# Two phase sums moved between the sixth and the seventh product, and a flag read ahead of the last work, in a gated linear attention with a cosine-gated layer

## The chip, the core and the metric

The kernel runs on one NeuronCore of a Trainium2 chip. The metric is the device time of one execution in microseconds (us), as a median over runs. All times below are in us unless marked ns. The engines are named as the profile names them: PE is TensorE's matmul and PEld its weight load, DVE is VectorE, ACT is ScalarE, POOL is GpSimd and SP is SyncE; a "q" behind the name marks the engine's sequencer or, for a DMA, the queue that issues it.

## The reference

Two blocks are computed one after the other. The first is a recurrence over 768 steps with a complex decay for each of 4 batches and 8 heads; the head size is 48:

```python
mag = np.sqrt(a_re * a_re + a_im * a_im)
scale = np.minimum(mag, 0.999) / (mag + 1e-06)
a_re_n, a_im_n = (a_re * scale, a_im * scale)
for t in range(S):
    ar, ai = (a_re_n[:, :, t, :, None], a_im_n[:, :, t, :, None])
    new_re = ar * S_re - ai * S_im
    new_im = ar * S_im + ai * S_re
    kv = np.einsum('bhd,bhe->bhde', k[:, :, t], v[:, :, t])
    S_re, S_im = (new_re + kv, new_im)
    y[:, :, t] = np.einsum('bhd,bhde->bhe', q[:, :, t], S_re)
```

Its result, as 3072 rows of 384 columns, goes through a layer with weights of 384 x 2048 and 2048 x 384:

```python
h = x @ w_in
g = h * np.cos(h)
return g @ w_out
```

## The kernel before

**Tiles and groups.** The steps are cut into chunks of 128 and two chunks make a group, so there are 12 groups (NG). One iteration n of the main loop in `fast_path` (from L1542 on) weaves three groups together: the scores, states and outputs of group n, the second matrix product of group n-1, and the decays, angles and keys of group n+1. The iteration ends with the first matrix product of group n (its "gate sums", named hp in the profile) and its gates.

**The angles of a group (n+1).** `log_steps` makes the logarithm and the angle of each decay on ScalarE and VectorE. `p_powers` and `g_phase` then sum them over the steps with matmuls by triangular matrices. `g_phase` (phs in the profile) does six matmuls for the two chunks of a group, then a cast on ScalarE and a subtraction on VectorE (both write tan). `keys` follows: `g_trig` (sine and cosine on ScalarE), `g_stack` (four products on VectorE: ks and qs), and `f_transpose` for the keys and then for the queries. Each `f_transpose` is one transpose on VectorE (tr), one copy to DRAM on SyncE's queue (moved) and the loads back: four for the keys (kT), one for the queries (qT). The transpose of the queries is put behind the first gate product of the previous group (`behind(turn, X[g - 1]["gated"])`). The next group's scores (sc) read kT and qT.

**The second product in seven.** From group 2 on (PLAIN) a group's second product is made as seven half-size products (`seventh`, p = 0 to 6, each in two parts of four j) after a Strassen-like scheme; `mixes` makes the mixed operands on VectorE. Products p = 0, 3, 5, 6 add into one PSUM tile (sum), the others use another (op). After each product ScalarE or VectorE adds it into the output tile ot. The product p = 6, the seventh, adds into sum, so it must wait until ScalarE has read out the state after p = 5, the sixth. In the last group p = 6 has a tile of its own (`alone`).

**What sets the order.** TensorE's matmuls are chained in the order in which the code calls them (`matmul` with `chain`). `weave` sorts the calls of an iteration by a number: each part spreads its items evenly over a span, as in

```python
(products(n - 1, 3, 7), 0.4, 0.56), (phases(n + 1), 0.472, 0.476),
(keys(n + 1), 0.5, 0.62), (quarters() if n == PLAIN else [], 0.4, 0.9),
```

so that both phases stand between the fifth product (its second part is at 0.47) and the sixth (at 0.49). In this stage VectorE's, ScalarE's and SyncE's instructions are ordered by a planner, which works with its own costs and takes what is ready, with the order of the code as priority; `behind` adds an edge that keeps one instruction after another on its engine. Each engine then runs its queue in order.

**The end.** `least`, `odd` and `wide` gather checks of the inputs' range. At the end of `tile_gateloop__then__act_gcu_kernel` (L1553 on) VectorE reduces them to one number for each partition, two DMAs write them into a line in DRAM, one reads the line back into one partition, VectorE reduces it to a flag, and every engine reads the flag (L1592) and branches on it (L1594). With the flag set the slow `general_path` would be run after all; with these inputs it is jumped over. All stores of the output are on SyncE's queue, so that SyncE reads the flag after the last store.

Of the kernel before, what the change touches and what calls it, by code (L numbers as in the profile page):

```python
# [11 lines left out]
F32 = mybir.dt.float32  # L12
U8 = mybir.dt.uint8
U32 = mybir.dt.uint32
I32 = mybir.dt.int32
# [4 lines left out]
ALU = mybir.AluOpType  # L20
AX = mybir.AxisListType
# [463 lines left out]


@with_exitstack
def fast_path(ctx, tc, q, k, v, a_re, a_im, moe_w_in, moe_w_out, out, least, odd, wide):

# [3 lines left out]
    nc = tc.nc  # L495
    B, H, S, D = q.shape
    DM, DF = moe_w_in.shape
    C = 128
# [3 lines left out]
    NG = N // G  # L502
    D2 = 2 * D
# [147 lines left out]
    late = {}  # L651
    tail = {}
# [33 lines left out]
    vector, scalar = Ordered(nc.vector, "vector"), Ordered(nc.scalar, "scalar")  # L686
# [424 lines left out]
    def quarters():  # L1111

        for name in "s1", "s2", "a22":
            right[name] = stage["pool"].tile([C, HJ, E2], F32, name="t_" + name)
        t1, t2, t4 = (right[name] for name in ("s1", "s2", "a22"))
        for j in range(0, HJ, 2):
            for t, a, b in (t1, b12, b11), (t2, b22, t1), (t4, b21, t2):
                yield lambda t=t, a=a, b=b, j=j: behind(vector.tensor_tensor(
                    out=t[:, ds(j, 2)], in0=a[:, ds(j, 2)], in1=b[:, ds(j, 2)],
                    op=ALU.subtract), Y[PLAIN * G]["masked"])  # L1120
# [28 lines left out]
    def seventh(g, p, part):  # L1149


        x, name = X[g], SEVEN[p]
        if p == 0 and part == 0:
            x["sum"] = pm.tile([C, E2], F32, tag="acc", name="sum", bufs=1)
            x["ot"] = [msb.tile([C, DM], F32, tag="ot", name="ot") for _ in range(G)]

        alone = g == NG - 1 and p == 6
        summed = p in (0, 3, 5, 6) and not alone
        if not summed and part == 0:
            x["op"] = pm.tile([C, E2], F32, tag="m", name="op", bufs=2)  # L1160
        ps = x["sum"] if summed else x["op"]
        for j in range(part * HJ // 2, (part + 1) * HJ // 2):
            matmul(ps, lhsT=left(g, name, j), rhs=right[name][:, j],
                   start=(j == 0 and (p == 0 or not summed)),
                   stop=(j == HJ - 1), skip_group_check=summed)
        if part == 0:
            return
        c11, c12, c21, c22 = (x["ot"][i][:, ts(half, E2)] for i in range(2) for half in range(2))
        if p in (0, 2, 5) or p == 6 and not alone:
            scalar.mul(out={0: c11, 2: c21, 5: c22, 6: c12}[p], in_=ps, mul=scale)  # L1170
        if g == NG - 1 and p == 5:
            scalar.mul(out=c12, in_=ps, mul=scale)
        if p in (1, 3, 4, 5) or alone:
            part_ = {1: c11, 3: c21, 4: c21, 5: c22, 6: c12}[p]
            added = vector.scalar_tensor_tensor(out=part_, in0=x["op"] if p == 5 else ps, scalar=scale,
                                                in1=part_, op0=ALU.mult, op1=ALU.add)
        row = g * G * C
        if g == NG - 1 and p == 1:
            nc.sync.dma_start(out=out[ds(row, C), 0:E2], in_=c11)
        elif p == 5:  # L1180
            late["out"] = added
            nc.sync.dma_start(out=out[ds(row + C, C), :], in_=x["ot"][1])
        elif p == 6:
            nc.sync.dma_start(out=out[ds(row, C), ds(alone * E2, DM - alone * E2)],
                              in_=c12 if alone else x["ot"][0])

    def products(g, lo, hi):
        if g < PLAIN:
            return []
        return [lambda p=p, part=part: seventh(g, p, part)  # L1190
                for p in range(lo, hi) for part in range(2)]

    def mixes(g, lo, hi):
        return [lambda p=p: mixed(g, p) for p in range(lo, hi)] if g >= PLAIN else []

    def weave(*parts):

        items = []
        for p, (part, lo, hi) in enumerate(parts):
            part = list(part)  # L1200
            items += [(lo + (hi - lo) * (i + 0.5) / len(part), p, t)
                      for i, t in enumerate(part)]
        for _, _, t in sorted(items, key=lambda x: x[:2]):
            t()
# [4 lines left out]
    def keys(g):  # L1209

        if not 0 <= g < NG:
            return
        for i, n in spans(g):
            yield lambda i=i, n=n: g_trig(g, i, n)
            yield lambda i=i, n=n: (g_stack(g, i, n), p_end(g, i, n))
            for name in "kT", "qT":
                if g >= PEG:
                    yield lambda i=i, n=n, name=name: f_transpose(g, i, n, name)
# [21 lines left out]
    def phases(g):  # L1240
        return [lambda i=i: g_phase(g, i) for i in range(G)] if 0 <= g < NG else []
# [299 lines left out]
    for n in range(2, NG):  # L1541
        weave((mixes(n - 1, 2, 4), 0.0, 0.12), (logs(n + 1), 0.0, 0.02), (chunks(n), 0.0, 0.36),  # L1542
              (upper[2:] if n == 2 else [], 0.0, 0.2), (products(n - 1, 0, 3), 0.0, 0.36),
              (prods(n + 1), 0.25, 0.27), (second(n - 1, 1), 0.36, 0.5),
              (products(n - 1, 3, 7), 0.4, 0.56), (phases(n + 1), 0.472, 0.476),
              (keys(n + 1), 0.5, 0.62), (quarters() if n == PLAIN else [], 0.4, 0.9),
              (last_quarter() if n == PLAIN else [], 0.9, 1.0), (first(n), 0.56, 1.0),
              (mixes(n, 0, 2), 0.9, 1.0), (guarded(n - 1, per) if n > 3 else [], 0.1, 0.9))
    weave((mixes(NG - 1, 2, 4), 0.0, 0.1), (products(NG - 1, 0, 7), 0.0, 1.0))
    assert not guards  # L1550
    return late
@with_exitstack
def kernel(ctx, tc, q, k, v, a_re, a_im, moe_w_in, moe_w_out, out):  # L1553

    nc = tc.nc
    D2, H = 2 * q.shape[3], q.shape[1]
    keep = ctx.enter_context(tc.tile_pool(name="keep", bufs=1))
    least = keep.tile([D2, 2 * H], F32, name="least")  # L1560
    C = 128
    NG, NJ = q.shape[0] * q.shape[2] // C // 2, moe_w_out.shape[0] // C
    odd = keep.tile([C, moe_w_in.shape[0] // C * 4 + NJ + NG + 1], F32, name="odd")
    wide = keep.tile([C, NG * NJ // 2], F32, name="wide")
    late = fast_path(tc, q, k, v, a_re, a_im, moe_w_in, moe_w_out, out, least, odd, wide)
    low = keep.tile([D2, 1], F32, name="low")
    nc.vector.tensor_reduce(out=low, in_=least, axis=AX.X, op=ALU.min)
    even = keep.tile([C, 1], F32, name="even")
    nc.vector.tensor_reduce(out=even, in_=odd, axis=AX.X, op=ALU.max)
    most = keep.tile([C, 1], F32, name="most")  # L1570
    nc.vector.tensor_reduce(out=most, in_=wide, axis=AX.X, op=ALU.max)
    nc.vector.tensor_scalar(out=even, in0=even, scalar1=0.0, scalar2=None, op0=ALU.is_le)
    nc.vector.tensor_scalar(out=most, in0=most, scalar1=2.4, scalar2=None, op0=ALU.is_le)
    nc.vector.tensor_tensor(out=even, in0=even, in1=most, op=ALU.mult)
    scratch = ctx.enter_context(tc.tile_pool(name="scratch", bufs=1,
                                             space=bass.MemoryType.DRAM))
    line_d = scratch.tile([D2 + C], F32, name="line_d")

    def behind(ins, other):
        tc.add_manual_dep(ins.ins, other.ins.name, mybir.DependencyInfo(  # L1580
            mybir.DependencyClass.NoSync, mybir.DependencyReason.DATA))

    behind(nc.sync.dma_start(out=line_d[0:D2], in_=low.rearrange("p o -> (p o)")),
           late["x"])
    nc.sync.dma_start(out=line_d[D2:D2 + C], in_=even.rearrange("p o -> (p o)"))
    line = keep.tile([1, D2 + C], F32, name="line")
    nc.sync.dma_start(out=line, in_=line_d.unsqueeze(0))
    bad = keep.tile([1, 2], F32, name="bad")
    behind(nc.vector.tensor_reduce(out=bad[:, 0:1], in_=line, axis=AX.X, op=ALU.min), late["out"])
    flag = keep.tile([1, 1], I32, name="flag")  # L1590
    nc.vector.tensor_scalar(out=flag, in0=bad[:, 0:1], scalar1=0.5, scalar2=None, op0=ALU.is_lt)
    taken = nc.values_load(flag[0:1, 0:1], min_val=0, max_val=1,  # L1592
                           skip_runtime_bounds_check_because="a comparison gives 0 or 1")
    with tc.If(taken > 0):  # L1594
        general_path(tc, q, k, v, a_re, a_im, moe_w_in, moe_w_out, out)


# [28 lines left out]
```

## Time and profile before

| | |
|---|---|
| median of 3 runs | 666.53 (664.78 to 667.04) |
| the profiled execution | 666.49 |
| its span, from the first to the last instruction | 664.7 |
| granted TensorE clock, mean | 0.996 |
| gate sums of one group (hp, 96 matmuls) | 20.7 |
| one of the seven products (16 matmuls) | 2.6 from start to start |
| both phase sums of a group (6 matmuls) | 1.05 |
| last matmul's end to the span's end | 6.8 |

The profile is one execution. Matmuls are pipelined and their ends are modelled, so the distance from the start of one product to the start of the next is the better measure of a product. A group of instructions is told as `line engine operation out<-in`, with the tiles by the program's names; as every matmul is issued in one helper, all stand on L689. A wait is put down to the instruction that released it. Reading the flag and branching are work of an engine's sequencer and are not counted as busy.

### The profile page before, as it was taken

Reading aid. Unit: us, or ns where it says so; the run is one execution under the profiler, and the core shown is the slowest. Engines: PE = TensorE matmul, PEld = TensorE weight load, DVE = VectorE, ACT = ScalarE, POOL = GpSimd, SP = SyncE. Lnnn points to the kernel's source line nnn. Section 1 sums busy time; section 2 is a strip of 40 time slices with the busy share of each in tenths; the row PEclk is TensorE's granted clock in tenths of the full one; section 3 lists DMA queues with packets and bytes.
Section 4 is the critical chain, followed back from the end, with each engine's and each line's share of the span. In section 5 each row is a group of like instructions: output and inputs, shape, how many; then the busy total and the mean of one; then the engine's idle time right before and its main releaser. Section 6 shows DMA issues by size and latency. Waiting matters only on the chain.

```text
span 664.7 us, 10764 instructions
## 1 busy us (share of the span) xinstructions
PE 644.0 (97%) x4077; PEld 575.7 (87%) x4077; DVE 491.7 (74%) x797; ACT 393.3 (59%) x728; POOL 28.0 (4%) x47
## 2 busy tenths in 40 slices
PE   7899999999999999999999999999999999999995
PEld 5788867767998999899899899898899899899895
DVE  4999989499788688688688688687688778762241
ACT  7888687284673593593594494495486486332330
POOL 2010200000000000010010010000000000000000
PEclk9999999999999999999999999999999999999998
DMA  9968755637628557657648637826927833533000
GB/s 245 207 190 215 211 170 120 166 64 186 132 48 209 124 145 190 143 139 170 166 126 188 164 100 163 214 72 146 240 80 164 206 94 96 164 98 96 25 6 25
DMA packets 233626, 94.90 MB, mean 143 GB/s; under 512 B 208846, under 2 KB 222033, under 8 KB 233564
## 3 DMA queue, kind: packets, MB, share of 16 engines
q1 hardware_dynamic: 227068, 68.62, 45.2%
q0 software_dynamic: 5632, 25.17, 11.4%
q8 instruction: 34, 0.56, 0.4%
q10 hardware_dynamic: 864, 0.33, 0.2%
q14 instruction: 28, 0.23, 0.1%
HBM read 69.28 MB, written 24.81 MB: 142 GB/s over the span
## 4 chain that ended last, share of the span: by engine, by line
PE 83%; DMA 5%; ACT 5%; DVE 5%; issue 1%; POOL 0%; DVEq 0%; SPq 0%; POOLq 0%
PE hp L689 37%; PE op L689 17%; PE sum L689 11%; PE sc L689 5%; PE yp L689 5%; PE sp L689 4%; DMA xT<-x 2%; PE phs L689 2%; DMA raw<-in_moe_w_out_dram 1%; ACT rs L709 1%; DVE tan L678 1%; PE lgs L689 1%; DVE mag L678 1%; ACT lo L709 1%; DMA x<-yT 1%
## 5 line engine op out<-in xcount | busy, mean ns | idle before, releaser
L689 PE MATMUL hp<-xT,w_in 128*128 128x256 f32 (+1 forms) x1176 | 252.7, 375 | 1.4 <-DMA xT<-x 1.4
L689 PEld LDWEIGHTS hp<-xT,w_in 128*128 128x128 f32 x1176 | 219.5, 190 | 32.2 <-DMA xT<-x 2.0
L709 ACT ACTIVATE gate<-hp,half_pi_b 128x512 f32<-128x512 f32 x96 | 66.0, 687 | 120.5 <-PE hp L689 120.5
L678 DVE TENSOR_TENSOR gate<-hp,gate 128x512 f32<-128x512 f32 x96 | 65.8, 685 | 70.3 <-ACT junk L678 69.8
L689 PE MATMUL op<-w_out,gate 128*128 128x192 f32 (+1 forms) x448 | 100.7, 374 | 0.0
L689 PEld LDWEIGHTS op<-w_out,gate 128*128 128x128 f32 x448 | 75.9, 190 | 16.9 <-issue 2.0
L678 ACT ACTIVATE junk<-hp 128x512 bf16<-128x512 f32 x96 | 56.6, 590 | 0.0
L689 PE MATMUL sum<-t_s,s 128*128 128x192 f32 x320 | 55.4, 326 | 0.2 <-DVE ot L678 0.2
L678 DVE TENSOR_TENSOR atm<-sc,causal 128x512 f32<-128x512 f32 x48 | 32.8, 687 | 30.0 <-PE sc L689 30.0
L689 PEld LDWEIGHTS sum<-t_s,s 128*128 128x128 f32 x320 | 52.6, 190 | 0.5 <-DVE ot L678 0.5
L689 PEld LDWEIGHTS sc<-qT,kT 96*128 96x128 f32 x384 | 47.7, 192 | 1.9 <-ACT qT L678 0.5
L689 PE MATMUL sc<-qT,kT 96*128 96x128 f32 x384 | 49.0, 275 | 0.2 <-ACT qT L678 0.2
L678 ACT ACTIVATE ot<-sum 128x192 f32<-128x192 f32 x30 | 9.5, 319 | 45.8 <-PE sum L689 45.8
L689 PE MATMUL yp<-atm,v 128*48 128x128 f32 x352 | 33.6, 277 | 1.1 <-DVE atm L678 1.1
L705 ACT ACT_TABLE_LOAD x24 | 30.8, 1283 | 4.0 <-DMA ident<-ident_const 3.6
L678 ACT CAST tan<-phs 128x384 int32<-128x384 f32 x24 | 11.4, 480 | 36.5 <-PE phs L689 36.5
L689 PE MATMUL sum<-w_out,s 128*128 128x192 f32 x144 | 25.8, 332 | 4.2 <-ACT ot L678 4.2
L689 PEld LDWEIGHTS sp<-v,ks 128*96 128x96 f32 x320 | 29.7, 165 | 0.0
L689 PE MATMUL yp<-qT,state 96*48 96x128 f32 x304 | 29.7, 272 | 0.0
L689 PE MATMUL sp<-v,ks 128*96 128x48 f32 x320 | 29.7, 245 | 0.0
L689 PE MATMUL sum<-w_out,gate 128*128 128x192 f32 x160 | 29.6, 329 | 0.0
L689 PEld LDWEIGHTS sum<-w_out,s 128*128 128x128 f32 x144 | 23.1, 190 | 6.9 <-ACT ot L678 6.9
(138 smaller groups left out, 976.2 us busy)
## 6 DMA issues: line engine op xcount, KB each, us to landing
moved<-tr SPq DMA_DIRECT2D x20, 768.0 KB
raw<-in_moe_w_in_dram POOLq DMA_DIRECT2D x16, 768.0 KB, 5.3
raw<-in_moe_w_out_dram POOLq DMA_DIRECT2D x16, 768.0 KB, 4.9
kT<-moved SPq DMA_DIRECT2D x40, 192.0 KB
qT<-moved SPq DMA_DIRECT2D x10, 768.0 KB
k<-in_k_dram SPq DMA_DIRECT2D x24, 192.0 KB
q<-in_q_dram SPq DMA_DIRECT2D x24, 192.0 KB
v<-in_v_dram SPq DMA_DIRECT2D x24, 192.0 KB
```

The costliest lines, as they stand in the source:

```text
L678: ins = getattr(self.engine, op)(**kw)
L689: chain(nc.tensor.matmul(out, **kw), "tensor")
L705: chain(nc.scalar.preload_act_table_set(table))
L709: chain(nc.scalar.activation(func=func, **kw))
```

## The change

It has two parts. In the main loop, for n = 3 to 10, the two phase sums are called between the sixth and the seventh product, and the keys' steps are called a little later; for n = 2 (PLAIN), where there are no seven products, all stays.

```diff
-              (products(n - 1, 3, 7), 0.4, 0.56), (phases(n + 1), 0.472, 0.476),
-              (keys(n + 1), 0.5, 0.62), (quarters() if n == PLAIN else [], 0.4, 0.9),
+              (products(n - 1, 3, 7), 0.4, 0.56),
+              (phases(n + 1), *((0.472, 0.476) if n == PLAIN else (0.516, 0.524))),
+              (keys(n + 1), *((0.5, 0.62) if n == PLAIN else (0.53, 0.64))),
+              (quarters() if n == PLAIN else [], 0.4, 0.9),
```

The second part is the end. The instructions that make the flag become a generator, `verdict`, which the last weave steps through: the line is made during the first product of the last group, the flag is made and read by all engines after the fourth, and TensorE's read is put behind the first half of the sixth. ScalarE's read is put behind its read-out of an earlier product, VectorE's last addition behind VectorE's read, SyncE's second-last store behind SyncE's read. The store of the first output quarter is put behind the line's read. The last store goes to ScalarE's queue, behind ScalarE's read. The branch itself stays where it was, after each engine's last instruction.

```diff
-    weave((mixes(NG - 1, 2, 4), 0.0, 0.1), (products(NG - 1, 0, 7), 0.0, 1.0))
+    checked = verdict(late)
+
+    def judged():
+        late["tensor"] = tail["tensor"]
+        next(checked, None)
+
+    weave((mixes(NG - 1, 2, 4), 0.0, 0.1), ([judged], 0.05, 0.15),
+          (products(NG - 1, 0, 7), 0.0, 1.0), ([judged], 0.58, 0.6), ([judged], 0.76, 0.8))
...
+            if alone:
+                behind(added, late["read DVE"])
+            late["vector"] = added
         row = g * G * C
         if g == NG - 1 and p == 1:
-            nc.sync.dma_start(out=out[ds(row, C), 0:E2], in_=c11)
+            behind(nc.sync.dma_start(out=out[ds(row, C), 0:E2], in_=c11), late["line"])
         elif p == 5:
-            late["out"] = added
-            nc.sync.dma_start(out=out[ds(row + C, C), :], in_=x["ot"][1])
+            put = nc.sync.dma_start(out=out[ds(row + C, C), :], in_=x["ot"][1])
+            if g == NG - 1:
+                behind(put, late["read SP"])
+        elif p == 6 and alone:
+            behind(nc.scalar.dma_start(out=out[ds(row, C), E2:DM], in_=c12),
+                   late["read Activation"])
         elif p == 6:
-            nc.sync.dma_start(out=out[ds(row, C), ds(alone * E2, DM - alone * E2)],
-                              in_=c12 if alone else x["ot"][0])
+            nc.sync.dma_start(out=out[ds(row, C), :], in_=x["ot"][0])
...
+    def verdict(late):
...
+        late["line"] = nc.sync.dma_start(out=line, in_=line_d.unsqueeze(0))
+        yield
+        bad = keep.tile([1, 2], F32, name="bad")
+        behind(nc.vector.tensor_reduce(out=bad[:, 0:1], in_=line, axis=AX.X, op=ALU.min),
+               late["vector"])
+        flag = keep.tile([1, 1], I32, name="flag")
+        nc.vector.tensor_scalar(out=flag, in0=bad[:, 0:1], scalar1=0.5, scalar2=None,
+                                op0=ALU.is_lt)
+        reads, values = nc.values_load_multi_w_load_instructions(
+            flag[0:1, 0:1], min_val=0, max_val=1,
+            skip_runtime_bounds_check_because="a comparison gives 0 or 1")
+        late["taken"] = values[0]
+        for ins in reads:
+            name = str(ins.ins.engine).split(".")[-1]
+            late["read " + name] = ins
+        behind(late["read Activation"], late["scalar"])
+        yield
+        behind(late["read PE"], late["tensor"])
+
+    late = fast_path(tc, q, k, v, a_re, a_im, moe_w_in, moe_w_out, out, least, odd, wide, verdict)
+    with tc.If(late["taken"] > 0):
         general_path(tc, q, k, v, a_re, a_im, moe_w_in, moe_w_out, out)
```

The instructions at the start of `verdict` (left out at its "...") are the same reductions, comparisons and DMAs that stood behind `fast_path` before.

More of the change, by code (lines that the diff above doesn't have):

```diff
@@ L487, in fast_path @@
 @with_exitstack
-def fast_path(ctx, tc, q, k, v, a_re, a_im, moe_w_in, moe_w_out, out, least, odd, wide):
+def fast_path(ctx, tc, q, k, v, a_re, a_im, moe_w_in, moe_w_out, out, least, odd, wide,
+              verdict):
     nc = tc.nc
@@ L1169, in seventh @@
         if p in (0, 2, 5) or p == 6 and not alone:
-            scalar.mul(out={0: c11, 2: c21, 5: c22, 6: c12}[p], in_=ps, mul=scale)
+            late["scalar"] = scalar.mul(out={0: c11, 2: c21, 5: c22, 6: c12}[p], in_=ps, mul=scale)
         if g == NG - 1 and p == 5:
@@ L1564 @@
     wide = keep.tile([C, NG * NJ // 2], F32, name="wide")
[L1565 to L1574, printed above, removed]
     scratch = ctx.enter_context(tc.tile_pool(name="scratch", bufs=1,
                                              space=bass.MemoryType.DRAM))
-    line_d = scratch.tile([D2 + C], F32, name="line_d")
     def behind(ins, other):
@@ L1581, in behind @@
             mybir.DependencyClass.NoSync, mybir.DependencyReason.DATA))
[L1583 to L1594, printed above, removed]
+    def verdict(late):
+        low = keep.tile([D2, 1], F32, name="low")
+        nc.vector.tensor_reduce(out=low, in_=least, axis=AX.X, op=ALU.min)
+        even = keep.tile([C, 1], F32, name="even")
+        nc.vector.tensor_reduce(out=even, in_=odd, axis=AX.X, op=ALU.max)
+        most = keep.tile([C, 1], F32, name="most")
+        nc.vector.tensor_reduce(out=most, in_=wide, axis=AX.X, op=ALU.max)
+        nc.vector.tensor_scalar(out=even, in0=even, scalar1=0.0, scalar2=None, op0=ALU.is_le)
+        nc.vector.tensor_scalar(out=most, in0=most, scalar1=2.4, scalar2=None, op0=ALU.is_le)
+        nc.vector.tensor_tensor(out=even, in0=even, in1=most, op=ALU.mult)
+        line_d = scratch.tile([D2 + C], F32, name="line_d")
+        behind(nc.sync.dma_start(out=line_d[0:D2], in_=low.rearrange("p o -> (p o)")),
+               late["x"])
+        nc.sync.dma_start(out=line_d[D2:D2 + C], in_=even.rearrange("p o -> (p o)"))
+        line = keep.tile([1, D2 + C], F32, name="line")
+        late["line"] = nc.sync.dma_start(out=line, in_=line_d.unsqueeze(0))
[16 more added lines that the diff above has]
+        behind(late["read PE"], late["tensor"])
```

## The prediction

> **What bounds the kernel now.** I read the page first (shares, then the chain that ended last), then the list of waits, then the timeline of one group and of the end.
>
> ```profile
> PE 644.0 (97%) x4077; PEld 575.7 (87%) x4077; DVE 491.7 (74%) x797; ACT 393.3 (59%) x728; POOL 28.0 (4%) x47
> PE 83%; DMA 5%; ACT 5%; DVE 5%; issue 1%; POOL 0%; DVEq 0%; SPq 0%; POOLq 0%
> ```
>
> TensorE is busy in 97% of the span and is 83% of the chain. So time is won only where TensorE stands still, or after its last matmul. The waits list names the stop between the sixth and the seventh product:
>
> ```profile
> PE sum L689 <- ACT ot L678: 4.2, 9, 0.5
> PE hp L689 <- DMA xT<-x: 1.4, 2, 1.2
> ```
>
> The timeline of one group (the iteration n=4) shows what surrounds it. The columns are start, duration, engine, line and operation; the wait stands at the end.
>
> ```profile
> 249.88 2.76 PE L689 MATMUL op<-w_out,gate 128*128 128x192 f32 x16
> 252.34 0.47 PE L689 MATMUL phs<-hi,exact 128*128 128x384 f32 x1
> ...
> 253.52 2.76 PE L689 MATMUL sum<-t_s,s 128*128 128x192 f32 x16
> ...
> 256.40 0.31 ACT L678 ACTIVATE ot<-sum 128x192 f32<-128x192 f32 x1
> ...
> 256.76 2.87 PE L689 MATMUL sum<-w_out,s 128*128 128x192 f32 x16 [0.48 <-ACT ot L678]
> ...
> 259.47 15.70 PE L689 MATMUL hp<-xT,w_in 128*128 128x256 f32 x72
> 259.53 2.25 DVE L678 STREAM_TRANSPOSE tr<-ks 128x1536 f32<-128x1536 f32 x1
> ...
> 264.16 2.24 DVE L678 STREAM_TRANSPOSE tr<-qs 128x1536 f32<-128x1536 f32 x1
> ...
> 271.58 2.66 SPq L926 DMA_DIRECT2D qT<-moved  x1
> ```
>
> The seventh product (256.76) adds into the bank that ScalarE must first read out (256.40). TensorE has nothing between. The two phase sums (six matmuls, 252.34 to 253.5) stand one product earlier. After the phases a long chain follows: angles, sines, stack, two transposes on VectorE, six DMAs on SyncE's queue, of which qT is last; the next group's first scores (280.19 here) need it.
>
> At the end, the view of the flag's load and branch (lines 1592 and 1594) shows durations in ns and start times:
>
> ```profile
> L1592 PEldq TENSOR_LOAD <-flag x1: 739/739/739, 656.6 to 656.6; - x1
> L1592 SPq TENSOR_LOAD <-flag x1: 521/521/521, 658.8 to 658.8; - x1
> L1594 PEldq COMPARE_BRANCH  x1: 3842/3842/3842, 657.4 to 657.4; - x1
> L1594 SPq COMPARE_BRANCH  x1: 45/45/45, 659.4 to 659.4; - x1
> L1594 SPq EVENT_SEMAPHORE  x8: 17/17/17, 662.5 to 663.0; - x8
> ```
>
> SyncE issues the last store at 658.42, reads the flag at 658.8, branches at 659.4, and its next instruction comes at 662.5: 3.0 us of nothing. Then follow 20 semaphore instructions (1.4) and the closing barrier. From the last matmul (657.9) to the span's end (664.7) it is 6.8 us.
>
> **What the Trainium skill says.** "Runtime: NRT & Kernel Launch", section Instruction fetch mechanics: a taken branch to a target outside the window that is held must fetch instructions by DMA first. The trace agrees: after their branches POOL, ACT, DVE and SP stand 2.5, 2.7, 3.1 and 3.0 us, and instruction blocks of 16 KB move meanwhile. "Advanced Engine Details and Errata", section Engine Queue Depths, gives TensorE's queue 64 entries. The trace shows part of it: the flag's load began on PE's sequencer at 656.58, when matmuls to 657.9 (16 instructions or more) were still to run. "PSUM — Partial Sum Buffer", section PSUM bank collisions, wants a semaphore between a reader and a writer of a bank; the 0.48 us above is such a wait.
>
> **The phases, step by step.** A product takes 2.60 us (start to start, 247.28 to 249.88). From 253.52 two products should end at 258.72, but the gate sums begin at 259.47. So the stop costs 0.75 with its restart. The phase sums take 1.05 wherever they stand. Placed in the stop, they give ScalarE 1.05 us for a read that was done 0.6 after the product; ScalarE has little else then, since the casts and sines of the angles now come later. Gain: up to 0.75 in each of eight groups (n=3 to 10; the waits list counts a ninth, n=11, which has no phases), 6.0 in all.
>
> The price is the chain behind the phases, which starts 2.60 later, and its cover is the slack at the next group's scores. From the trace's semaphore records qT lands at 279.38 and the scores begin at 280.19: slack 0.81. For n=3 to 10 it is 1.75, 0.81, 1.35, 1.65, 2.14, 1.49, 0.92, 1.56. As the gain also moves the scores forward by 0.75, a group's net is -0.75 + max(0, D + 0.75 - slack), where D is how much later qT lands.
>
> D is not 2.60, since part of the chain waits anyway. Phases end at 256.29 instead of 253.69. VectorE's first transpose followed 5.84 after them, of which 0.27 was the addition of the sixth product, now done before: it runs 261.86 to 264.1. The first gate product, ready at 263.56 - 0.75 = 262.8, follows to 264.75, and the second transpose, which the code holds behind that gate, runs to 267.0, against 266.4 before. The first transpose's copy lands 3.3 us after its issue (261.80 to 265.06), so at 267.4, and the kT loads start then instead of at 266.85. D = 0.6. VectorE's lateness has cover: the fourth gate sum (266.5) needs the buffer that the first gate product frees (264.75).
>
> Exceptions: at n=8 the gate sums wait for xT (465.20 landed, 465.24 begun), so nothing is gained; at n=5 xT leaves 0.71. At n=10 SyncE has the kT loads ahead of the second copy, and D could be 2.3 (+0.8); put the other way round it gains 0.75: I take 0. With D = 0.6: -0.75, -0.21, -0.71, -0.75, -0.75, 0, -0.32, 0: sum **-3.5**. Bounds: D = 0.35 (the case at n=8, where an earlier DMA held SyncE) gives -4.7, D = 1.3 (VectorE half a microsecond slower) about -0.2.
>
> **The flag and the last store.** The same eight small VectorE instructions and three DMAs (two writes into a line, one read) are moved, none is removed. They ran beside products at 641.7 to 650 already, costing TensorE nothing. The store of the first quarter is now queued behind the line's read on SyncE: 645.40 becomes about 650.2; only the end waits for it, and it lands before the last ones. The line lands at 652.88; its reduction waited until 656.00 for the sixth product's addition, and now runs at about 652.9.
>
> The loads of the flag then start some 0.57 later, at 653.5. ACT (0.66), DVE (0.54), SP (0.52) and POOL (0.72) have nothing queued behind theirs before 655.4: cost nothing. TensorE's load stands between the halves of the sixth product, which starts at 652.56, so its first half ends at 653.86. Behind the load are queued 24 matmuls and their weights. The load ends at 653.5 + 0.74 = 654.2 at a line as late as now: a stop of 0.3 to 0.65. A line earlier by 1 us (no store in its way) means none. I take 0.3.
>
> After the last matmul: the addition ends 0.47 later (658.39). SyncE's work ends at 656.5 with the second-last store, so its fetch is over by 659.5. VectorE branches at 658.1 instead of 658.7, over by 661.2. ScalarE issues the last store at 658.4 (0.44, as its DMAs at the start took), branches at 658.9 and with its 2.74 goes on at 661.6. The store lands by 661.0, as now. ScalarE is last; its own semaphore, SyncE's last ones and the barrier end 1.1 later, at about 662.75 instead of 664.7: -1.95. With TensorE's stop: **-1.65**. Bounds: -2.3 (no stop, a quicker fetch as POOL's 2.5) and -0.6 (stop 0.65 and a fetch of 3.5).
>
> **Sum.** The profiled execution took 666.49, 1.8 around its span of 664.7; the median of the runs is 666.53, the same. 666.49 - 3.5 - 1.65 = **661.4**; the bounds give 659.5 to 665.7 for this case.
>
> **Rivals.** *The transposes come after the gate.* If VectorE's queue has the first gate product ahead of the first transpose, the latter runs 263.4 to 265.7, its copy lands at 269.0, the second ends at 267.9 and kT starts 2.2 to 2.6 later. TensorE then waits for qT in each group. With D = 2.3: +0.55, 1.49, 0.95, 0.65, 0.16, 0.81, 1.38, 0.74, sum +6.7, and with the end's gain +5.0: 671.5. It decides from D of about 1.65 on, where the groups' loss eats the end's gain. For it: the two are only 0.95 apart in readiness, and the order is a planner's. Against: the transpose is ready first, and before it was ahead by 4. *The stop stays.* If ScalarE's queue has a cast of a phase ahead of the read of the sum, the read ends 1.5 after the product, the seventh waits 0.5 beyond the phases, and only the end gains: 664.8. Against: the read is ready first by half a microsecond. *The end gives nothing.* The load starves TensorE by 0.65 and ScalarE's fetch is as slow as TensorE's 3.84: the end keeps about 0.2, total 662.8.
>
> **Chances.** Likeliest 0.62, transposes behind the gate 0.18, the stop stays 0.10, the end gives nothing 0.10. Range 659.0 to 669.5: it holds all but the worse part of the first rival (D above 2.0) and a gain beyond the bounds. Some 0.3% (2 us) is what a measurement of this kernel can tell from no change. Faster than 664.5: 0.57 of the likeliest, 0.03 and 0.08 of the last two, 0.68; slower than 668.5: 0.14 of the first rival; the rest, 0.18, between.
>
> **What would show it.** Right: no wait of sum on ACT's ot but one, phs between the sums, qT's issue some 0.6 later, scores that wait little, a branch on SP near 656.5, an end some 4.9 after the last matmul. Wrong: a new wait of sc on a DMA of 1 us or more in most groups, a PE gap at the load beyond 0.7, or the 0.48 still there.

## The result and the profile after

The changed kernel takes 660.68 us (median of 22 runs, 658.18 to 667.46), the kernel before 665.77 us in 22 runs on the same chip: ratio 0.9921, 95% interval 0.9902 to 0.9941. It is faster by 5.1 us.

The ratios leave out each kernel's slow runs, so they are not just the quotient of the medians, and some executions begin the main loop 5 to 8 us late (the profiled one of the changed kernel, 667.46 us with a span of 665.7, does), so stretches are counted below from the first gate sums of n=2 (164.41 us after, 156.44 before) to the end.

The page after: the shares of the engines, the granted clock in 40 slices (the 6 in the third falls in the late beginning), and the chain that ended last.

```profile
PE 650.7 (98%) x4077; PEld 582.8 (88%) x4077; DVE 490.6 (74%) x797; ACT 393.5 (59%) x728; POOL 27.9 (4%) x47
...
PEclk9969999999999999999999999999999999999999
...
PE 79%; DMA 7%; DVE 6%; ACT 2%; SPq 2%; issue 2%; POOL 0%; DVEq 0%; POOLq 0%
```

TensorE is still the bound. The list of TensorE's waits after (total, times, longest) has changed where the change was made:

```profile
PE hp L690 <- DMA xT<-x: 0.9, 1, 0.9
...
PE sum L690 <- ACT ot L679: 0.4, 1, 0.4
PE sc L690 <- DMA qT<-moved: 0.3, 1, 0.3
```

Of the nine stops of a sum behind ScalarE's read-out, the eight of n=3 to 10 are gone; the one of n=11 is left. The scores wait anew for qT, 0.28 us at 540.28 (and 0.14 at 388.12, which this list leaves out). The timeline of n=4 after shows the new order (start, duration, engine, line, operation, the idle time before in brackets):

```profile
257.38 2.76 PE L690 MATMUL op<-w_out,gate 128*128 128x192 f32 x16
...
259.98 2.76 PE L690 MATMUL sum<-t_s,s 128*128 128x192 f32 x16
...
262.44 0.47 PE L690 MATMUL phs<-hi,exact 128*128 128x384 f32 x1
...
262.78 0.33 ACT L679 ACTIVATE ot<-sum 128x192 f32<-128x192 f32 x1 [5.78 <-PE sum L690]
...
263.62 2.76 PE L690 MATMUL sum<-w_out,s 128*128 128x192 f32 x16
...
266.22 10.09 PE L690 MATMUL hp<-xT,w_in 128*128 128x256 f32 x46
...
269.36 2.25 DVE L679 STREAM_TRANSPOSE tr<-ks 128x1536 f32<-128x1536 f32 x1
...
271.58 0.68 DVE L679 TENSOR_TENSOR gate<-hp,gate 128x512 f32<-128x512 f32 x1
...
272.19 2.23 DVE L679 STREAM_TRANSPOSE tr<-qs 128x1536 f32<-128x1536 f32 x1
```

The phase sums fill 262.44 to 263.6 while ScalarE reads the sum out (262.78 to 263.11), and the seventh product starts with nothing shown ahead of it. From 259.98, two products of 2.60 and the phases' 1.05 should end at 266.23; the gate sums begin at 266.22, so nothing is lost between. The first transpose still goes ahead of the first gate product, the second behind it.

At the end, the flag's loads and branches after, in ns with start times:

```profile
L1612 SPq TENSOR_LOAD <-flag x1: 482/482/482, 656.1 to 656.1; - x1
...
L1612 PEldq TENSOR_LOAD <-flag x1: 492/492/492, 657.3 to 657.3; - x1
L1612 ACTq TENSOR_LOAD <-flag x1: 471/471/471, 657.9 to 657.9; - x1
```

```profile
L1624 SPq EVENT_SEMAPHORE  x8: 17/17/17, 662.1 to 663.1; - x8
...
L1624 SPq COMPARE_BRANCH  x1: 45/45/45, 659.0 to 659.0; - x1
...
L1624 ACTq COMPARE_BRANCH  x1: 54/54/54, 661.3 to 661.3; - x1
...
L1624 ACTq EVENT_SEMAPHORE  x1: 17/17/17, 664.7 to 664.7; - x1
```

SyncE now branches at 659.0, before TensorE's last matmul ends (660.40), and goes on at 662.1. ScalarE issues the last store at 660.90, branches at 661.3 and goes on at 664.7: it is now last.

Where the time went, from each profile. "n=3-10" is from the gate sums of n=2 to those of n=10; "n=11 on" from there to the last matmul's end; the tail is the rest of the span.

| kernel (main loop's beginning) | n=3-10 | n=11 on | tail | sum |
|---|---|---|---|---|
| before (156.44) | 412.26 | 89.23 | 6.79 | 508.27 |
| before, second profile (164.66) | 411.93 | 92.08 | 6.72 | 510.73 |
| after (164.41) | 407.05 | 88.95 | 5.27 | 501.27 |
| after, second profile (162.81) | 407.98 | 88.92 | 5.41 | 502.31 |
| phases alone (156.24) | 409.90 | 92.31 | 6.82 | 509.03 |
| end alone (156.32) | 411.93 | 89.19 | 4.62 | 505.74 |
| own tile, phases as before (163.59) | 406.37 | 90.23 | 4.75 | 501.35 |
| low's write later (156.26) | 408.16 | 87.77 | 5.10 | 501.03 |
| last store on SyncE (156.27) | 407.94 | 90.18 | 6.87 | 504.99 |
| transposes behind the gate (162.70) | 416.53 | 90.78 | 4.74 | 512.05 |
| own tile, low's write later (163.82) | 406.04 | 87.09 | 5.40 | 498.53 |
| no branch (160.96) | 408.20 | 92.28 | 3.10 | 503.58 |

From before to after the eight groups give 5.2 us, n=11 on 0.3, the tail 1.5.

### The profile page after: what moved, and what is told of

The parts are those of the page before. It is cut to its first block, busy times and chain, and to the rows that moved or that the text cites. A ratio compares the mean times of both kernels' runs of the same rounds, so it can differ in the third digit from the quotient of the medians.

```text
span 665.7 us, 10771 instructions
## 1 busy us (share of the span) xinstructions
PE 650.7 (98%) x4077; PEld 582.8 (88%) x4077; DVE 490.6 (74%) x797; ACT 393.5 (59%) x728; POOL 27.9 (4%) x47
## 4 chain that ended last, share of the span: by engine, by line
PE 79%; DMA 7%; DVE 6%; ACT 2%; SPq 2%; issue 2%; POOL 0%; DVEq 0%; POOLq 0%
PE hp L690 31%; PE op L690 17%; PE sum L690 13%; PE sc L690 5%; PE yp L690 5%; PE sp L690 3%; PE phs L690 2%; DMA qT<-moved 2%; SPq L925 2%; PE lgs L690 1%; DMA raw<-in_moe_w_out_dram 1%; DMA xT<-x 1%; DVE mag L679 1%; PE yr L690 1%; DVE qs L679 1%
## 5 line engine op out<-in xcount | busy, mean ns | idle before, releaser
L690 PE MATMUL hp<-xT,w_in 128*128 128x256 f32 (+1 forms) x1176 | 255.3, 378 | 0.9 <-DMA xT<-x 0.9
L690 PEld LDWEIGHTS hp<-xT,w_in 128*128 128x128 f32 x1176 | 222.2, 193 | 31.9 <-DMA xT<-x 1.4
L679 DVE SCALAR_TENSOR_TENSOR ot<-op,ot 128x192 f32<-128x192 f32 x31 | 11.0, 355 | 33.8 <-ACT ot L679 24.8
L690 PE MATMUL op<-t_a,gate 128*128 128x192 f32 x160 | 29.0, 332 | 0.0
L679 ACT COPY yT<-yp 48x512 f32<-48x512 f32 x44 | 25.3, 574 | 4.7 <-PE yp L690 4.3
```

The costliest lines, as they stand in the source:

```text
L679: ins = getattr(self.engine, op)(**kw)
L690: chain(nc.tensor.matmul(out, **kw), "tensor")
```

## The experiments

The theory: filling the stop in eight groups gives some 3.5 us, less than the stop cost because qT's lateness gives part back; the early flag and ScalarE's queue give about 1.65. The rivals: one part does it all, the order of the transposes decides, or the stop could have been removed for more without moving the phases.

The experiments ran on several chips, so each is to be read by its ratio to the kernel before on its own chip. There the kernel before takes 671.34 us beside the phases alone, the end alone, the own tile and low's later write, and 669.48 beside the other four.

### Each part alone

The phases alone: the kernel before with the first hunk of the diff.

```diff
-              (products(n - 1, 3, 7), 0.4, 0.56), (phases(n + 1), 0.472, 0.476),
-              (keys(n + 1), 0.5, 0.62), (quarters() if n == PLAIN else [], 0.4, 0.9),
+              (products(n - 1, 3, 7), 0.4, 0.56),
+              (phases(n + 1), *((0.472, 0.476) if n == PLAIN else (0.516, 0.524))),
+              (keys(n + 1), *((0.5, 0.62) if n == PLAIN else (0.53, 0.64))),
+              (quarters() if n == PLAIN else [], 0.4, 0.9),
```

> The kernel before with the phases and keys moved, the end as before. Theory (each stop of 0.75 us before the seventh product is filled, the chain behind the phases is covered by the slack at the next scores): 3.5 to 5.5 us less than before, ratio 0.992 to 0.995; the wait of sum on ACT's ot falls from 9 to 1; the end stays at 6.8 us after the last matmul. Rival (the gain of the change is mostly the end): less than 2 us, ratio above 0.997.

Measured 666.73 us, ratio 0.9937 (0.9905 to 0.9969). In its profile n=3-10 takes 409.90, 2.4 us less than before; n=11 on takes 3.1 us more than before: 1.6 of that is a longer wait for xT (2.8 us against 1.2), and 1.5 lies after n=11's gate sums have begun, where the page's row of the granted clock shows an 8 among the nines. So this one execution is no faster than before from n=2 on; the gain of the whole kernel stands on its 22 runs.

The profile also shows a cost of moving the phases that the prediction did not count. At n=8 the sixth product waits for VectorE's addition, before and with the phases alone:

```profile
458.87 2.87 PE L689 MATMUL sum<-t_s,s 128*128 128x192 f32 x16 [0.21 <-DVE ot L678]
```

```profile
455.73 2.54 PE L689 MATMUL sum<-t_s,s 128*128 128x192 f32 x14 [1.04 <-DVE ot L678]
```

In their old place the phases stood ahead of this product and covered most of VectorE's lateness. In the kernel with the last store on SyncE the same wait is 1.25.

The end alone: the changed kernel without that hunk, by the same lines turned round.

> The changed kernel with the phases and keys put back to their old places, so only the end is changed. Theory: 1.5 us less than before (6.8 us after the last matmul become 5.3), ratio about 0.9975; nine stops of 0.48 us before the seventh product. Rival (the gain is mostly the end): 4 us or more, ratio below 0.994.

Measured 667.16 us, ratio 0.9957 (0.9926 to 0.9988). Its groups stand as before (411.93) and its tail is 4.62. Both parts gain. That the whole needs both is read from the profiles, where each part shortens its own stretch; the intervals of the ratios overlap with that of the whole (0.9902 to 0.9941).

### A tile of its own instead of filler

In the end-alone kernel the seventh product gets a PSUM tile of its own in every group, as the last group has it already, so that it need not wait for ScalarE at all. For that ScalarE copies the sum once more and VectorE adds the product. The phases stay where they were.

```diff
-        alone = g == NG - 1 and p == 6
+        alone = p == 6
...
-        if p in (0, 2, 5) or p == 6 and not alone:
+        if p in (0, 2, 5):
...
-        if g == NG - 1 and p == 5:
+        if p == 5:
...
-            if alone:
+            if alone and g == NG - 1:
...
-        elif p == 6 and alone:
+        elif p == 6 and g == NG - 1:
```

> The end as changed, phases and keys at their old places, but in every group the seventh product adds into a PSUM tile of its own, as it does in the last group, so that it waits for nobody; ScalarE copies the sum once more and VectorE does the addition. Theory (the stop itself was the cost): the stops of 0.48 us are gone with nothing put into them; 0.75 us in seven groups (not in the one that waits for xT) and 1.5 at the end, 6 to 7 us less than before, ratio 0.990 to 0.991, and qT comes early, with no new wait for it. Rival (the phases' move gained through the new order of VectorE's and SyncE's queues, not through the stop): only the end's 1.5 us, ratio 0.9975.

Measured 662.71 us, ratio 0.989 (0.9832 to 0.9948). The head of TensorE's waits in this kernel:

```profile
PE hp L690 <- DMA xT<-x: 3.1, 2, 2.9
PE yr L690 <- DVE state L679: 2.3, 1, 2.3
...
PE sc L690 <- ACT qT L679: 0.2, 1, 0.2
```

No sum waits for ScalarE and no score for the DMA of qT. The eight groups gain 412.26 - 406.37 = 5.9 us on the kernel before, 0.74 a group on the mean (0.52 to 1.13 in single ones), and 5.6 on the end-alone kernel. This is what the stop cost, measured without a filler, but the 1.13 of n=8 is not the stop's alone: there a load came sooner (see n=8 below). Without n=8 it is 0.68 a group, near the 0.75 of the prediction. Filling the stop with the phases gains 4.1 to 5.2 in the five profiles that have the early flag too, and 2.4 in the phases alone; without n=8 it is 2.2 to 4.3, against 4.8 with the own tile. Part of the difference is new waits of the scores for qT (0 to 1.3 us in all, by the execution).

### The last group's xT

In the last group SyncE issues a write of 96 values of 4 bytes (low into line_d) right behind the xT load. The timeline after:

```profile
612.09 0.38 SPq L1046 DMA_DIRECT2D xT<-x  x1
612.52 0.47 SPq L1600 DMA_DIRECT2D line_d<-low  x1
621.22 0.94 PEld L690 LDWEIGHTS hp<-xT,w_in 128*128 128x128 f32 x5 [1.20 <-DMA xT<-x]
621.22 1.13 PE L690 MATMUL hp<-xT,w_in 128*128 128x256 f32 x4 [0.90 <-DMA xT<-x]
```

This xT takes 9.1 us to land; in the other groups it takes 3.6 to 4.3. The experiment holds that write back behind the store of the seventh product of the last group but one, in the changed kernel:

```diff
-            nc.sync.dma_start(out=out[ds(row, C), :], in_=x["ot"][0])
+            late["put"] = nc.sync.dma_start(out=out[ds(row, C), :], in_=x["ot"][0])
...
-               late["x"])
+               late["put"])
```

> The changed kernel, with the small write of the line's first part (96 values of 4 bytes) put behind the store of the seventh product of the last group but one, so that it no longer runs beside the last load of xT. Theory (that write makes xT's load of the last group take 9 us in place of 4, and TensorE wait 0.9 us for it): xT lands within 4.5 us of its issue, the wait of hp is gone, about 0.9 us less than the changed kernel, ratio to before 0.990 to 0.991. Rival (xT's load is slow in the last group for another reason): as the changed kernel, 0.992, with the wait still there.

Measured 661.31 us, ratio 0.988 (0.9823 to 0.9936). The wait is gone, xT lands 4.7 us before it is needed, and n=11's group takes 48.69 instead of 49.76. Over all profiles the last xT takes 9.0 to 11.0 us in the ten that have the write right behind it, and 3.3 and 3.4 in the two that have it later.

### The store's queue

The changed kernel with the last store back on SyncE's queue; the flag stays early.

```diff
-            behind(nc.scalar.dma_start(out=out[ds(row, C), E2:DM], in_=c12),
-                   late["read Activation"])
+            nc.sync.dma_start(out=out[ds(row, C), E2:DM], in_=c12)
```

> The changed kernel with the last store back on SyncE's queue; the flag is still read early. Theory (what the end gains is that fewer fetches after a branch and fewer semaphore steps stand behind the last store): SyncE stores, branches, fetches 3.05 us and then has its 20 semaphore instructions (1.4) and the barrier (0.8) to do, so 6.2 us from the last matmul to the end, against 4.6 to 5.3 with the store on ScalarE and 6.8 before: the early flag alone is worth 0.6, the other queue about 1.2. Rival (the early flag is all): 4.6 to 5.3 as changed.

Measured 666.43 us, ratio 0.9938 (0.9906 to 0.997). The branches of SyncE and ScalarE in this kernel:

```profile
L1623 SPq EVENT_SEMAPHORE  x8: 17/17/17, 659.0 to 659.6; - x8
...
L1623 SPq COMPARE_BRANCH  x1: 45/45/45, 655.3 to 655.3; - x1
L1623 ACTq EVENT_SEMAPHORE  x1: 17/17/17, 655.5 to 655.5; - x1
```

SyncE must issue the last store (654.88) before it branches, and then stands 3.7 us, longer than in the kernel before (3.05). So the tail is 6.87, no shorter than before (6.79). What the two steps save shows when the standstill of the engine that branches last is taken off each tail:

| kernels | branches last | tail less its standstill |
|---|---|---|
| before (two profiles), phases alone | SyncE | 3.74 |
| last store on SyncE, early flag | SyncE | 3.15 |
| last store on ScalarE, early flag (seven profiles) | ScalarE | 1.93 |

Each value holds within 0.01 in all profiles of its row. The early flag saves 0.6 and the store's queue 1.2, as was expected. After its branch SyncE has 25 sequencer instructions to do, ScalarE 5. The rest of a tail is how long the last engine stood in that execution, 2.7 to 3.7 us. The ratio alone does not separate this kernel from the changed one.

### Both transposes behind the gate

This makes the first rival of the prediction true in the changed kernel: the rule that holds the second transpose behind the first gate product now holds both.

```diff
-        if name == "qT" and "gated" in X[g - 1]:
+        if "gated" in X[g - 1]:
```

> The changed kernel with the transpose of the keys, too, put behind the first gate product of the group, the order that the prediction's first rival feared. Theory (the price of moving the phases is how late qT lands, against the slack at the scores): the first transpose starts 1.6 us later, kT and qT follow by as much, TensorE waits for qT in most groups, 0.5 to 1.6 us each, 6 to 7 in all: the loop of eight groups gives back all of its gain, ratio to before 0.998 to 1.002. Rival (qT's lateness is absorbed elsewhere, the slack isn't a limit): as the changed kernel, 0.992.

Measured 671.06 us, ratio 1.0027 (0.9998 to 1.0056). TensorE's waits and, from the timeline, the first scores after n=7's gate sums:

```profile
PE sc L690 <- DMA qT<-moved: 5.3, 5, 2.0
...
PE sum L690 <- DVE ot L679: 1.3, 2, 0.7
```

```profile
425.96 0.69 DVE L679 TENSOR_TENSOR gate<-hp,gate 128x512 f32<-128x512 f32 x1 [0.94 <-ACT junk L679]
426.57 2.24 DVE L679 STREAM_TRANSPOSE tr<-ks 128x1536 f32<-128x1536 f32 x1
428.74 2.23 DVE L679 STREAM_TRANSPOSE tr<-qs 128x1536 f32<-128x1536 f32 x1
...
444.46 1.13 PE L690 MATMUL sc<-qT,kT 96*128 96x128 f32 x8 [1.70 <-DMA qT<-moved]
```

The eight groups take 416.53, 4.3 us more than before and 9.5 more than after, and the stops of the scores add up to 7.0. The rival's mechanism holds. Its price was too high: it put the groups at 6.7 more than before and the whole at 5.0 more, and by the interval the whole is at most 3.7 more. The changed kernel did not take that way because its first transpose was ready before the gate product.

### Without the branch

The changed kernel without the conditional and the general path; the fallback for the cases that the flag reports is left out. The flag is still made, but nothing needs its value, and the trace has no loads of it: at their line only semaphore instructions are left.

```diff
-    with tc.If(late["taken"] > 0):
-        general_path(tc, q, k, v, a_re, a_im, moe_w_in, moe_w_out, out)
```

> The changed kernel without the branch and the general path behind it (the fallback for inputs out of range is left out; the flag is still made and read). Theory (what is left of the end is one fetch after ScalarE's branch): the end is then set by the last store's landing, 2.2 us after its issue, then SyncE's semaphores and the barrier: 3.7 to 4.2 us from the last matmul to the end against 4.6 to 5.3. Rival (the end is set by the store's landing already): unchanged, 4.6 or more.

Measured 664.67 us, ratio 0.9917 (0.9884 to 0.995). The tail is 3.10, below what was expected: the last store lands 1.65 us after its issue, and nothing but it and the closing semaphores is left. Against tails of 4.6 to 5.4, some 1.5 to 2.3 us of the end are still one engine's standstill after its branch; the missing loads have no part in it, as in the changed kernel the last of them ends at 658.8, before the last matmul. The median does not show the gain plainly. The profiled execution lost in other places: TensorE waits 1.93 us for xT in n=11, and from there it takes 41.49 to the last matmul where the changed kernel takes 39.19, with an 8 in the row of the granted clock. In this kernel TensorE's wait for the flag stands between the halves of the sixth product, and TensorE stops 0.38 us there.

### The two together

The own tile with the phases as before, and low's write held back: both edits above on the end-alone kernel.

> The kernel with a tile of its own for the seventh product, phases at their old place, and the small write of the line's first part put behind the store of the last group but one. Theory (both waits are independent): the stops are gone as in the kernel with the own tile, and its wait of 2.9 us for xT in the last group too, so some 3 us less than that kernel, 8 to 9.5 less than before, ratio 0.986 to 0.988, the fastest so far. Rival (xT in the last group is late for lack of bandwidth, not for the small write): ratio 0.990, the wait stays.

Measured 661.44 us on a chip on which the kernel before takes 669.48: ratio 0.9854 (0.9794 to 0.9915), the lowest ratio of all. Its list of TensorE's waits has no sum behind ScalarE, no xT and no DMA of qT in it; the head:

```profile
PE busy L690 <- DVE one_b L541: 1.5, 1, 1.5
PE phs L690 <- ACT tan L710: 1.3, 2, 0.9
PE lgs L690 <- DVE lg L679: 1.3, 2, 0.7
```

From the gate sums of n=2 on it takes 498.53, 2.7 less than the changed kernel and 9.7 less than before. Its interval and that of the changed kernel (0.9902 to 0.9941) overlap; the two were not timed beside each other.

### n=8 in more profiles

The changed kernel gained 1.55 us at n=8, where nothing was predicted. In the kernel before, VectorE's queue stands there behind the weights' DMA. On SyncE's queue a write that waits for VectorE (row) stands ahead of the DMAs that make x and load xT, so that xT comes late too:

```profile
454.39 0.57 DVE L678 TENSOR_SCALAR raw<-raw 128x768 uint32<-128x768 uint32 x1 [3.06 <-DMA raw<-in_moe_w_out_dram]
```

In the changed kernel the same wait is a third of that:

```profile
457.65 0.56 DVE L679 TENSOR_SCALAR raw<-raw 128x768 uint32<-128x768 uint32 x1 [0.94 <-DMA raw<-in_moe_w_out_dram]
```

Yet two other kernels with the same main loop, the phases alone and the last store on SyncE, waited 2.84 and 3.05 and gained only 0.16 and 0.02 at n=8. So both kernels were profiled once more, unedited.

> The changed kernel once more, unedited, for a second look at one execution. The open point is the group n=8, where the changed kernel gained 1.55 us in its first profile against 0.16 and 0.02 in two other kernels with the same main loop, and where VectorE's queue stood 0.94 us behind the weights' DMA against 2.84 and 3.05. Theory A: the wait belongs to the execution (it was long, 2.7 to 3.06, in four executions whose main loop began at 156 us, and shorter, 0.94 to 2.12, in four that began at 161 to 164; one at 156 had 1.54). Then this execution shows about 3 us of wait, some 51.7 us for n=8 and 458 to 460 us from the gate sums of n=2 to those of n=11 if it begins at 156, or about 1 us, 50.2 and 456.8 if it begins late. Theory B: the change itself shortens the wait, so that it is about 1 us in any execution of this kernel. The end after the last matmul should be 4.6 to 5.3 us either way.

> The kernel before once more, unedited, beside it. Its first profile began its main loop at 156.44 us, waited 3.06 us for the weights' DMA at n=8 and took 462.3 us from the gate sums of n=2 to those of n=11. Theory A (the wait belongs to the execution): the same again if it begins at 156, but a wait of 1 to 2 us, about 50.9 us for n=8 and some 461 us in all if it begins late. Theory B (the wait belongs to the order of the kernel before): about 3 us and 51.8 us for n=8 either way. The end after the last matmul 6.8 us.

One run each, 666.91 and 677.17 us at a mean granted clock of 0.991 and 0.986, beside one of the kernel before with 669.83 at 0.996; only their stretches are used here. Both began late. The changed kernel waited 1.06 us again and took 50.74 for n=8; the kernel before waited 3.04 and took 51.43. The late beginning is thus not what shortens the wait: that form of theory A falls. Theory B isn't shown either: with the stop gone the wait was 0.94, 1.06, 1.20, 1.47, 1.54, 2.12, 2.84 and 3.05 in eight executions (the kernel with the transposes behind the gate aside); with the stop, 2.71, 3.04 and 3.06 in three. The trace's semaphore records show where it varies. The load is issued at the same place of the loop (9.9 us after the one before it, 9.2 in one), the first of its 16 shares lands 4.0 to 4.5 us later in all of them, and the last 4.7 to 6.9 later. Its packets show the place. Most take 0.23 us. In each of the five profiles with a wait of 2.7 or more, one packet that starts 2.8 to 3.7 us after the issue takes 1.0 to 1.3; in the five with 0.94 to 1.54, none that starts so late takes over 0.5. What holds this packet was not found, since the records do not name a packet's DMA engine; a collision with SyncE's loads, which the change shifts, would fit.

## Why the prediction was right

The predicted 661.4 stands beside 660.68. Both parts gained by the mechanism that was foretold; that the sum came within a microsecond is in part luck, since terms that were missed offset each other. The terms, one by one:

| period of n | predicted | after | after, second profile |
|---|---|---|---|
| 3 | -0.75 | -0.48 | -0.48 |
| 4 | -0.75 | -0.74 | -0.74 |
| 5 | -0.17 | -0.40 | -0.11 |
| 6 | -0.75 | -0.64 | -0.74 |
| 7 | -0.75 | -0.34 | -0.12 |
| 8 | 0 | -1.55 | -1.04 |
| 9 | -0.75 | -0.83 | -0.83 |
| 10 | -0.32 | -0.24 | -0.23 |
| 11 | +0.75 | -0.28 | -0.31 |
| sum | -3.5 | -5.5 | -4.6 |

A period runs from the gate sums of n-1 to those of n; measured is its length less that of the kernel before in its first profile. The prediction booked a late qT with the group whose chain it is. Its loss falls at the scores of the next period, so it is moved there: 0.54 from n=4 to 5, 0.43 from n=9 to 10, and the 0.75 by which n=10 was set to nothing, to 11. The sum stays the same.

- **The stop costs 0.75 a group:** right. The own tile gained 0.75 at n=3, 9 and 10, and 0.68 on the mean without n=8. The wait that the profile shows (0.48) is less than two thirds of 0.75.
- **The phases fill it, and ScalarE reads in time:** right, as the timeline shows; the stop at n=11 stayed, as counted.
- **The first transpose stays ahead of the first gate product:** right. It begins 5.57 us after the phases' end, as worked out, and the second follows behind the gate.
- **D = 0.6:** right for kT, too high for qT. Counted from where the phases would have ended in their old place, kT's loads start 0.52 to 0.72 us later in six of the eight groups, 2.25 later at n=10 (the 2.3 that was feared) and 0.67 earlier at n=8. qT itself took less time to land: its own lateness spread from -1.3 to +1.2 with a mean near zero, and its mean is 0.2 to 0.4 in the other five profiles with the phases moved and the transposes free. Single DMAs are not foreseen to half a microsecond.
- **Where the scores would wait:** right in place. For 0.54 after n=4 the two profiles of the changed kernel show 0 and 0.40; for 0.43 after n=9, 0.28 and 0.28. Waits that were not foreseen came after n=6 (0.14 and 0.37) and n=7 (0 and 0.28).
- **n=5 limited by xT:** near. xT has 0.04 us to spare there after the change, 0.33 in the second profile, and TensorE does not wait for it in either.
- **n=8 bound by xT, no gain:** wrong in both profiles of the changed kernel, right in the phases alone and with the last store on SyncE (0.16 and 0.02). What made xT late there was the weights' DMA in VectorE's queue, which in the changed kernel held it about 2 us less. With 1.0 to 1.6 us it is the largest term that the sum missed; without n=8 the sums are -3.9 and -3.6, beside the predicted -3.5.
- **n=10 taken as 0:** too low. The planner set the second copy ahead of the kT loads, the better of the two orders left open; qT did not come late, and the period of n=11 lost nothing.
- **The price of the first rival, 671.5:** too high, though its loss came at the first scores as foretold. Forced, it gave 671.06, but where the kernel before takes 669.48; 671.5 meant 5.0 more than before. The kT loads came 2.25 later on the mean, inside the 2.2 to 2.6 that were taken, but qT landed only 1.5 later, not 2.3. The turning point at 1.65 is not borne out either: with qT 1.5 late the groups lost 4.3, more than the end gains.
- **TensorE's stop of 0.3 at its flag load:** wrong, it was 0. The load begins 0.30 us before the seventh product and the branch follows it by 0.1 us, while all of that product's matmuls run on without a gap; so the load stood behind the last of them, where nothing waits for it. Why it was put there the record does not show. Where the wait does stand between the halves, in the kernel without the branch, the stop is 0.38. (The prediction also counted 16 instructions or more that were still to run at the load before; the trace has 13 that start after it, and 33 after the change.)
- **The line lands up to 1 us earlier:** wrong. It landed 13.5 us after the first product's start, 13.3 before. Not the first store but its own write of 128 values of 4 bytes, 6.5 us to land (645.95 to 652.42), sets it.
- **The end -1.95 before that stop:** right in kind, 0.4 too much in the profile: ScalarE stood 3.35 us after its branch, not 2.74, so that the tail fell by 1.5 (3.5 and 1.3 in the second profiles). In the end-alone kernel, where ScalarE stood 2.7, it fell by 2.2. The two errors at the end nearly cancel: -1.65 was predicted, -1.3 to -1.5 came.

From the gate sums of n=2 on the first profiles differ by 7.0 us, the second ones by 8.4 (of which 2.9 is that the kernel before waited 1.2 longer for xT than in its first profile and was slower after it), the medians by 5.1 (3.9 to 6.5 by the interval). A profile is one execution; how much of n=8's gain most executions have is not settled, and with it how much of the near hit is luck.

## What to carry to other kernels

A wait in the list can understate what a stop of TensorE costs: measure start to start over it (0.75 for a wait of 0.48), and then ask whether the dependence can go instead of being filled. Without n=8 the own tile gained 4.7 and 4.8 us in the groups in its two profiles, the filler 2.2 to 4.3; the moved phases had also covered another wait in their old place. At a kernel's end, let the engine with the least to do after the branch issue the last store (1.2 us here), and read the flag early (0.6). Compare such ends with the last engine's standstill taken off, since it varies by 1 us between executions. And price a forced rival against the kernel before on the same chip, not against a time from another.

## What the runs showed of the hardware

- After its branch past the general path an engine stood 2.5 to 4.0 us until its next instruction, and the same engine differed between executions: SyncE 2.7 to 3.7, ScalarE 2.6 to 3.5, VectorE 2.8 to 3.2, and TensorE 3.4 to 4.0, where the branch's own record lasts that long. Instruction blocks move meanwhile (two of 16 KB and eight of 8 KB at the end of the kernel before); that the fetch is what an engine stands for is not shown by a run of its own.
- Writes of 4 bytes each are slow beyond their size: 128 of them took 6.3 to 7.2 us to land, and 96 of them right behind a load of 384 KB on the same queue came with 9.0 to 11.0 us for that load, in ten profiles; with the write moved away it took 3.3 and 3.4.
- The last of a load's 16 shares landed up to 2.8 us after the first, in some executions at the very same place of the loop and in others within 0.4; in the five profiles where it was latest (6.5 us or more after the issue), a packet had taken 1.0 to 1.3 us instead of 0.23.
